# Norm statistics one unit earlier, x^T chunks and residual rows requested one at a time, last stores on three queues

## The chip, the cores and the metric

One Trainium2 chip, one of its cores. The metric is the device time of one execution in microseconds (us). Before the change it is 900.78 us, the median of three runs (899.95 to 901.37).

## The reference

The inputs are q, k and v of shape (4 batches, 8 heads, 768 positions, 64), 16 centroids for each head, and the weights of a two-layer block, all float32 by the time they are used (the block's weights arrive as float64).

```python
q_n, k_n, c_n = (t / (norm(t, axis=-1) + 1e-6) for t in (q, k, centroids))
q_assign = argmax(einsum('bhsd,hcd->bhsc', q_n, c_n), -1)
k_assign = argmax(einsum('bhsd,hcd->bhsc', k_n, c_n), -1)
scores = where(q_assign[..., :, None] == k_assign[..., None, :], q @ k^T / sqrt(64), -1e9)
x = softmax(scores) @ v                      # heads side by side: (4, 768, 512)
mu, var = mean(x, -1), mean((x - mu)**2, -1)
xn = (x - mu) / sqrt(var + 1e-6) * g_ln
out = x + maximum(xn @ w_ch1, 0) @ w_ch2     # 512 -> 2048 -> 512
```

## The kernel before

The kernel has two stages. The first, up to about 329 us of the span, is attention for 16 pairs of heads. It leaves two copies of x in device memory: transposed (`xT_d`, features by positions) and by rows (`x_d`). The change does not touch it. The second stage is the block, one batch `b` (0 to 3) after the other.

*The block.* Products with `w_ch1` (first layer) and `w_ch2` (second layer) are done with seven products of half-size blocks in place of eight, so between the TensorE products there are sums of blocks on VectorE. The first layer of a batch is cut into eight units `j` of about 9 us, each with seven products (`first_layer(b, j, part)`, its matmuls at L803). From batch 1 on the second layer does this twice over (`deep_layer`): seven outer products `m`, in the order 4, 7, 1, 6, 5, 2, 3, each of seven inner ones (`way`), makes 49 steps of 1.3 us, with the matmuls at L1093. The list `STEPS` gives their order; two ways of an outer product come after the first ways of the next: (4,1) (4,2) (4,6) (4,5) (4,7) (7,1) (7,2) (4,4) (4,3) (7,6) (7,5) (7,7) (1,1) (1,2) (7,4) (7,3) (1,6) and so on. In batch 1 deep steps begin at 544.0 us, in batch 2 at 683.9 us, in batch 3 at 820.5 us. The last two products of the first layer (parts 4 and 3 of unit 7) stand after (4,1) and (4,2).

*The weights of the deep steps* come from device memory, 256 KB for each step, through a ring of ten slots in SBUF (`ring_load`, L1035). Step number i uses slot i modulo 10. Ten loads are issued at the ends of units 5, 6 and 7 (four, four, two), and after that one load follows each step. Where a load reads from shows in the trace: `w_d` and `w_t` hold sums of blocks, `w_all` plain blocks. Steps (1,1) and (1,2) are numbers 12 and 13 and the first that read `w_all`.

*The queues.* The order of TensorE, VectorE, ScalarE and of SyncE's queue (SP) is the order of the program text, so a DMA that has to wait on SP holds all later ones. SP issues nearly all DMAs of this stage; ScalarE's queue helps only with output stores of the last batch. SP's and ScalarE's DMAs share eight semaphores in turn, so that the ninth DMA waits until the first of the nine has landed. POOL's queue is idle from about 400 us on.

*Work for batch b+1 inside batch b.* The end of unit `j` is `unit_end(b, j)`. Batch b+1's row statistics are taken there for b+1 of 2 and 3: `rows_load` (L526) fetches 128 rows of `x_d` into one of two buffers, `norm_rows` takes their mean and variance with two ScalarE passes. One of the six row tiles is done at the end of each of the units 1 to 6. `norm_stats` (end of unit 6) takes the root on ScalarE and the reciprocal on VectorE. `norm_stat_rows` (end of unit 7) turns the 12 x 128 statistics on TensorE (L569), copies them out (L573), stores them to `stat_d` (L574) and reads them back twice, spread over all partitions, as `stat_row` (L577, 384 KB each). In batch 1 `w2_split` stores a 1 MB operand to `w_d` at the end of the units 0 to 6 (L1011). Then come the ring loads of that unit's end.

In the deep layer `between()`, called after step (4,2), asks for the transposed x of batch b (`rest_load`, 768 KB, L1137), which VectorE adds to the output (`add_rest`, L1143, first used after step (4,3)), and for the four chunks of the transposed x of batch b+1 (`norm_load`, 384 KB each, L521). VectorE subtracts the mean row from chunk 0 after step (4,4), from chunk 1 after (7,5), from chunk 2 after (1,3), from chunk 3 after (6,6) (`norm_apply`, L584). The table `jobs` holds which of these calls follows which step.

*The end.* In the last batch the outer product 3 is turned and stored piece by piece. `last_part` (L1191 transposes, L1195 stores) acts after the ways 2, 7, 4 and 3, with four stores each, alternately on ScalarE's and SP's queue. After the last instruction of each engine's program come a load of a flag (L1438) and a branch (L1439) over a general path that is not taken with these inputs, and a barrier in which POOL collects the other engines (L1632).

Of the kernel before, what the change touches and what calls it, by code (L numbers as in the profile page):

```python
# [19 lines left out]
def kernel(  # L20
# [11 lines left out]
    nc = tc.nc  # L32
    B, H, S, D = q.shape
# [3 lines left out]
    NT = S // P  # L37
# [5 lines left out]
    NDC = DM // P  # L43
# [167 lines left out]
    NDH, NFH = NDC // 2, NFC // 2  # L211
# [303 lines left out]
            normed[b] = [xpool.tile([P, NDC, S], F32, tag="xn", name="xn")]  # L515
        return normed[b]

    def norm_load(b):
        xn = norm_tiles(b)[0]
        for c in range(NDC):  # L520
            nc.sync.dma_start(out=xn[:, c, :], in_=xT_d[b][c])  # L521

    def rows_load(b, t):
# [173 lines left out]
    with tc.manual_schedule(engines=order | {mybir.EngineType.Pool}):  # L697
        for u in range(len(pairs) * slots):
            n, slot = divmod(u, slots)
# [378 lines left out]
    def unit(name):  # L1078
        return units.tile([P, 2, HC], F32, tag="unit", name=name, bufs=6)
# [51 lines left out]
    def rest_load(b, k):  # L1131

        if b + 1 == B and k:
            t = xpool.tile([P, 3, S], F32, tag="sums", name="rest_x", bufs=2)[:, :2]
        else:
            t = units.tile([P, 2, S], F32, tag="rest", name="rest_x", bufs=1)
        nc.sync.dma_start(out=t, in_=xT_d[b][2 * k : 2 * k + 2].rearrange("h p s -> p h s"))  # L1137
        rest_x[b, k] = t
# [32 lines left out]
    def deep_layer(b, more, st):  # L1171

        done = {}

        def ahead_of(m):
            p = st[m] = {}
            onto = {2: 1, 3: 5}.get(m)
            p["add"] = done.get(onto)
            p["to"] = done[m] = done[onto] if onto else unit(f"m{m}")

        def sum_onto(i, j):
            nc.vector.tensor_tensor(done[i], done[i], done[j], ALU.add)

        def last_part(o, way):

            part = {2: (0, 0), 7: (1, 1), 4: (1, 0), 3: (0, 1)}.get(way)
            if part is None:
                return
            r, j = part
            y = unit("y_end")[:, 0, :QC]  # L1190
            nc.vector.transpose(y, o[:, j].rearrange("p (t a r) -> p t a r", a=2, r=Q)[:, :, r])  # L1191
            to = out[b].rearrange("(a r t) m -> a (r t) m", r=Q, t=NT)[r]
            for i in range(P // Q):
                m = MH + j * P + i * Q
                (nc.scalar, nc.sync)[i % 2].dma_start(  # L1195
                    out=to[:, m : m + Q], in_=y[i * Q : (i + 1) * Q].rearrange("r (t f) -> r t f", f=Q)
                )

        def between():
            first_layer(b, NFH - 1, 3)  # L1200
            relu(len(summed))
            outer_sums(NFH - 1, True)
            rest_load(b, 0)
            if more:
                norm_load(b + 1)
            else:
                rest_load(b, 1)

        def s4(n):
            return lambda: outer_late((1, 1), (0, 1), "s", n)  # L1210

        def norm(i, c):
            return lambda: norm_apply(b + 1, i, c)

        def rest(r, k, m):
            return lambda: add_rest(b, r, k, done[m])

        def out_of(r, k, m):
            return lambda: turn(b, r, k, done[m])

        def onto(i, j):
            return lambda: sum_onto(i, j)

        jobs = {
            (4, 1): [lambda: first_layer(b, NFH - 1, 4)],
            (4, 2): [between],
            (4, 3): [rest(1, 0, 4)],
            (7, 6): [s4(0)], (7, 4): [s4(1)], (7, 3): [s4(2)], (1, 6): [s4(3)],
            (1, 4): [onto(4, 7)], (6, 3): [onto(6, 1)],
            (5, 4): [onto(4, 6)], (5, 3): [onto(5, 6)], (2, 6): [onto(7, 5)],  # L1230
        }
        for i, m in enumerate(ORDER[1:]):
            for n, way in enumerate((5, 7)):
                jobs[ORDER[i], way] = [lambda m=m, n=n: inner_sums(st, m, (n,))]
        if more:
            for at, (i, c) in (
                ((4, 4), (0, 0)), ((7, 5), (0, 1)), ((1, 3), (0, 2)), ((6, 6), (0, 3)),
                ((6, 5), (1, 0)), ((6, 4), (1, 1)), ((5, 6), (1, 2)), ((5, 5), (1, 3)),
            ):
                jobs.setdefault(at, []).append(norm(i, c))  # L1240
            jobs[2, 4] = [out_of(1, 0, 4)]
            jobs[2, 3] = [rest(0, 0, 2), lambda: rest_load(b, 1)]
            jobs[3, 6] = [lambda: x_sum(b + 1, 1)]
            jobs[3, 5] = [lambda: w1_sums(b + 1, 0, (0, 1))]
            jobs[3, 4] = [lambda: x_sum(b + 1, 2)]
            later(
                rest(1, 1, 7), out_of(1, 1, 7), out_of(0, 0, 2), None,
                rest(0, 1, 3), out_of(0, 1, 3), None,
            )
        else:  # L1250
            jobs[1, 3] = [rest(1, 1, 7)]
            jobs[5, 6] = [rest(0, 0, 1), onto(4, 6)]
            del jobs[5, 4]
            jobs[2, 5].append(rest(0, 1, 5))
            jobs[2, 1] = [out_of(1, 0, 4)]
            jobs[2, 7].append(out_of(1, 1, 7))
            jobs[2, 3] = [out_of(0, 0, 2)]

        for m, way in STEPS:
            if way == 1:  # L1260
                ahead_of(m)
            deep_product(st, m, way)
            ring_load(b)
            leave(2 if more else 4, (nc.sync,) if more else (nc.sync, nc.scalar))
            if way == 1:
                inner_late(st, m, way)
            for job in jobs.get((m, way), ()):
                job()
            if way == 2:
                inner_late(st, m, way)  # L1270
            if m == 3 and not more:
                last_part(done[m], way)
        leave(len(leaving))
        places[1, 1], places["e"] = places["e"], places[1, 1]
# [91 lines left out]
    with tc.manual_schedule(engines=order | {mybir.EngineType.SP}):  # L1366
        first.close()
        splits = first.enter_context(tc.tile_pool(name="splits", bufs=1))
        outer = {}

        def unit_end(b, j):

            if b + 1 < B:
                if j == 0:
                    rows_load(b + 1, 1)
                elif j <= NT:
                    norm_rows(b + 1, j - 1)
            if b == 1:
                if j == 0:
                    outer["ends"] = all_in_range()  # L1380
                if j == 2:
                    outer["flag"] = flag_of(outer.pop("ends"))
                m = (1, 5, 3, 4, 2, 7, 6, None)[j]
                if m in SUMS:
                    w2_split(m, outer.pop("t"))
                elif m:
                    w2_split(m, by_half(w2_block(*{1: (0, 0), 2: (1, 0), 3: (1, 1)}[m])))
                if j in (1, 3, 5):
                    outer["t"] = w2_back({1: 4, 3: 3, 5: 2}[j])
                if j in (5, 6):  # L1390
                    outer_late("s", "e", (0, 0), j - 5)
            while pending:
                job = pending.pop(0)
                if job is None:
                    break
                job()
            if b + 1 < B and j + 2 == NFH:
                norm_stats(b + 1)
            if b + 1 < B and j + 1 == NFH:
                norm_stat_rows(b + 1)  # L1400
            leave(4)
            if j > 4:
                for _ in range(4):
                    if ring["next"] < len(STEPS) * (b - 1) + RING:
                        ring_load(b)

        for b in range(1, B):
            deep[b] = {}
            if b + 1 < B:
                rows_load(b + 1, 0)  # L1410
            if b == 1:
                outer["t"] = w2_back(1)
                first_units(b, 0)
            else:
                first_layer(b, 0, 1)
                first_layer(b, 0, 2)
                first_layer(b, 0, 6)
                relu(1)
                w1_sums(b, 0, (2, 3))
                x_sum(b, 3)  # L1420
                first_layer(b, 0, 5)
                first_layer(b, 0, 7)
                x_sum(b, 4)
                w1_sums(b, 1)
            unit_end(b, 0)
            for j in range(1, NFH):
                first_units(b, j)
                unit_end(b, j)
            relu(len(summed))
            inner_sums(deep[b], ORDER[0], cs=slice(NQH - 1, NQH))  # L1430
            if b == 1:
                first.close()
                units = pool("units", 1)
            deep_layer(b, b + 1 < B, deep[b])
        flag = outer["flag"]
# [201 lines left out]
```

## Time and profile before

| what | value |
|---|---|
| time, median of three runs | 900.78 us (899.95 to 901.37) |
| the profiled execution's own time | 897.76 us |
| its span, from first to last instruction | 896.0 us |
| TensorE busy | 879.3 us, 98% of the span |
| VectorE busy | 701.6 us, 78% |
| ScalarE busy | 400.1 us, 45% |
| POOL busy | 77.9 us, 9% |
| granted TensorE clock, mean | 0.998 |
| last matmul ends | 887.65 us |

The profiled execution is a single one, and it is 3.0 us under the median; 1.76 us of its time lies outside the span. TensorE's busy time is modelled for the ends of matmuls, but its gaps can be read: where a matmul starts later than the one before it ended, the waits name who released it. "SPq", "ACTq" and "POOLq" are the instructions of the queues of SyncE, ScalarE and POOL; their length is the time to issue a DMA, not the time to its landing. Lines are those of the kernel before.

### The profile page before, as it was taken

What the parts mean: (1) busy time and instruction counts of PE and PEld (TensorE: products, weight loads), DVE (VectorE), ACT (ScalarE), POOL (GpSimd) and SP (SyncE); (2) the same over time, 40 slices, a digit from 0 to 9 for tenths busy, and PEclk for the clock granted to TensorE, in tenths of its full rate; (3) what the DMA queues carried; (4) which work ended last, traced back from release to release, by engine and by line L of the source; (5) the groups of instructions that cost most, each with busy time, mean ns of one, the idle gap of its engine ahead of it and who ended that gap; (6) DMA issues with size and microseconds to landing.
All of it is one profiled execution on the core that took longest, in us unless ns stands there. A gap on an engine that the chain in (4) does not pass through costs nothing.

```text
span 896.0 us, 13278 instructions
## 1 busy us (share of the span) xinstructions
PE 879.3 (98%) x4724; PEld 576.4 (64%) x4724; DVE 701.6 (78%) x1158; ACT 400.1 (45%) x739; POOL 77.9 (9%) x141
## 2 busy tenths in 40 slices
PE   8999999999999999999999999899999999999996
PEld 4444444444444445568886558897557997556995
DVE  6999999999889879889545677897646897655775
ACT  4777777999877743331003552101553101333110
POOL 1122222121112112110000000000000000000000
PEclk9999999999999999999999999999999999999999
DMA  7789899999898446877513668863243872421775
GB/s 160 156 179 175 161 183 190 211 193 181 168 201 148 125 97 185 201 180 243 181 55 119 215 214 284 286 187 77 50 121 130 306 204 60 88 83 60 242 198 104
DMA packets 250841, 147.86 MB, mean 165 GB/s; under 512 B 193952, under 2 KB 209424, under 8 KB 249744
## 3 DMA queue, kind: packets, MB, share of 16 engines
q1 hardware_dynamic: 234992, 130.77, 55.8%
q0 software_dynamic: 7712, 14.99, 8.4%
q10 hardware_dynamic: 8064, 1.18, 0.8%
q8 instruction: 39, 0.64, 0.3%
q14 instruction: 34, 0.28, 0.1%
HBM read 105.25 MB, written 33.25 MB: 155 GB/s over the span
## 4 chain that ended last, share of the span: by engine, by line
PE 62%; DMA 2%; DVE 0%; SPq 0%; issue 0%; ACT 0%
PE x_ps L803 18%; PE x_ps L1093 11%; PE z_ps L803 9%; PE z_ps L1093 6%; PE x_ps L910 5%; PE y_ps L803 5%; PE y_ps L1093 3%; PE z_ps L910 2%; PE y_ps L910 1%; PE s_ps L386 1%; DMA w<-w_all 1%; PE a_ps L398 1%; DMA w<-w_d 1%; DMA stat_d<-st 0%; PE den_ps L452 0%; DVE u L1108 0%
## 5 line engine op out<-in xcount | busy, mean ns | idle before, releaser
L381 ACT ACTIVATE e<-s_ps 128x768 f32<-128x768 f32 x192 | 151.7, 812 | 9.3 <-PE s_ps L386 4.6
L386 PE MATMUL s_ps<-t,t 64*128 64x384 f32 x768 | 154.9, 483 | 0.0
L398 PE MATMUL a_ps<-e,v_sb 128*64 128x384 f32 x768 | 130.9, 491 | 0.0
L398 PEld LDWEIGHTS a_ps<-e,v_sb 128*64 128x64 f32 x768 | 52.3, 137 | 75.7 <-issue 62.8
L386 PEld LDWEIGHTS s_ps<-t,t 64*128 64x128 f32 x768 | 68.2, 188 | 35.1 <-issue 34.2
L1093 PE MATMUL x_ps<-lower,w 128*128 128x192 f32 x448 | 81.2, 327 | 3.4 <-DMA w<-w_all 2.5
L1093 PEld LDWEIGHTS x_ps<-lower,w 128*128 128x128 f32 x448 | 73.9, 190 | 5.7 <-DMA w<-w_all 2.8
L834 DVE TENSOR_TENSOR lower<-z_ps,u 128x384 f32<-128x384 f32 x56 | 31.0, 553 | 54.5 <-PE z_ps L803 45.7
L386 PE MATMUL s_ps<-mask,mask 64*128 64x384 bf16 x384 | 63.0, 324 | 1.1 <-ACT e L381 0.7
L842 ACT ACTIVATE lower<-lower 128x384 f32<-128x384 f32 x88 | 45.0, 522 | 41.2 <-DVE lower L834 41.2
L433 DVE TENSOR_TENSOR two<-e 128x1536 f32<-128x1536 f32 x30 | 52.5, 1751 | 12.9 <-ACT e L381 12.7
L829 ACT COPY u<-x_ps 128x384 f32<-128x384 f32 x64 | 30.6, 478 | 67.6 <-PE x_ps L803 67.6
L829 ACT COPY p<-x_ps 128x384 f32<-128x384 f32 x32 | 15.0, 470 | 91.2 <-PE x_ps L803 91.2
L436 DVE TENSOR_TENSOR two<-two,e 128x1536 f32<-128x1536 f32 x30 | 52.5, 1750 | 1.7
L803 PE MATMUL x_ps<-xn,w 128*128 128x384 f32 x128 | 46.6, 487 | 0.0
L803 PE MATMUL x_ps<-xn,ws 128*128 128x384 f32 x128 | 46.5, 486 | 0.0
L803 PE MATMUL z_ps<-xt,ws 128*128 128x384 f32 x128 | 46.5, 486 | 0.0
L803 PE MATMUL x_ps<-xt,ws 128*128 128x384 f32 x128 | 46.5, 486 | 0.0
L803 PE MATMUL z_ps<-xn,ws 128*128 128x384 f32 x128 | 46.5, 486 | 0.0
L803 PE MATMUL y_ps<-xn,w 128*128 128x384 f32 x128 | 46.5, 486 | 0.0
L803 PE MATMUL x_ps<-xt,w 128*128 128x384 f32 x128 | 46.5, 486 | 0.0
L386 PEld LDWEIGHTS <-mask 64*128 64x128 bf16 x384 | 19.2, 94 | 42.3 <-issue 11.3
(209 smaller groups left out, 1484.7 us busy)
## 6 DMA issues: line engine op xcount, KB each, us to landing
w<-w_d SPq DMA_DIRECT2D x84, 256.0 KB, 3.4
raw<-in_moe_w_ch_dram SPq DMA_DIRECT2D x32, 512.0 KB, 5.2
w<-w_t SPq DMA_DIRECT2D x36, 256.0 KB, 4.9
w<-tb POOLq DMA_DIRECT2D x32, 256.0 KB, 6.4
w_d<-wt SPq DMA_DIRECT2D x7, 1024.0 KB, 5.1
w<-w_all SPq DMA_DIRECT2D x27, 256.0 KB, 3.2
v_sb<-in_v_dram SPq DMA_DIRECT2D x32, 192.0 KB, 5.4
xr<-x_d SPq DMA_DIRECT2D x24, 256.0 KB, 3.0
```

Source lines behind the costliest of these rows:

```text
L381: nc.scalar.activation(e, s[:, :, :HC], AF.Exp, scale=SCALE)
L386: nc.tensor.matmul(s[:, j, :HC], of_keys[:, keys], of_queries[:, o : o + HC], start=part == first, stop=part != first, skip_group_check=True,)
L398: nc.tensor.matmul(acc[j * D : (j + 1) * D, :HC], loaded[n]["v"][:, j, c, :], e[:, j, :], start=(c == 0), stop=(c == NT - 1),)
L433: nc.vector.tensor_tensor(two, soft.pop(u), soft.pop(u + 1), ALU.add)
L436: nc.vector.tensor_tensor(two, two, soft.pop(u + 2), ALU.add)
L803: nc.tensor.matmul(bank[:, :HC], lhs[:, c, :], rhs[:, c], start=first and c == 0, stop=c == NDH - 1, skip_group_check=True,)
L829: nc.scalar.copy(t, bank[:, :HC])
L834: nc.vector.tensor_tensor(h, bank[:, :HC], other, ALU.add)
L842: nc.scalar.activation(h, h, AF.Relu)
L910: nc.tensor.matmul(bank[:, :MH].rearrange("p (h f) -> p h f", h=2), hidden[lhs + (c,)][:, tt * P : (tt + 1) * P], rhs[:, :, c], start=firs ...
L1093: nc.tensor.matmul(bank, w[:, c, :], a[:, c], start=way in (1, 2, 5) and c == 0, stop=c == NQH - 1, skip_group_check=True,)
```

## The change

1. Statistics one unit earlier. `norm_rows(b+1, j)` runs at the end of unit j in place of j+1 (0 to 5 in place of 1 to 6), `norm_stats` at the end of unit 5 in place of 6, `norm_stat_rows` at the end of unit 6 in place of 7.
2. Requests one by one. `between()` asks for chunk 0 alone. Chunk 1 is requested after step (4,7), chunk 2 after (7,2), chunk 3 after (7,3). `rest_load(b, 0)` moves from (4,2) to (4,5); in the last batch `rest_load(b, 1)` moves from (4,2) to (7,2).
3. Last stores. Of the stores of the last outer product, way 7 uses SP, ScalarE, POOL, SP and way 4 ScalarE, POOL, SP, ScalarE; ways 2 and 3 start with SP.

No arithmetic is changed. Each engine has as many instructions as before, save the two stores that go from SP and ScalarE to POOL.

```diff
-    def norm_load(b):
+    def norm_load(b, *chunks):
         xn = norm_tiles(b)[0]
-        for c in range(NDC):
+        for c in chunks or range(NDC):
             nc.sync.dma_start(out=xn[:, c, :], in_=xT_d[b][c])
...
             r, j = part
+            queues = {
+                7: (nc.sync, nc.scalar, nc.gpsimd, nc.sync), 4: (nc.scalar, nc.gpsimd, nc.sync, nc.scalar),
+            }.get(way, (nc.sync, nc.scalar))
...
-                (nc.scalar, nc.sync)[i % 2].dma_start(
+                queues[i % len(queues)].dma_start(
...
             outer_sums(NFH - 1, True)
-            rest_load(b, 0)
             if more:
-                norm_load(b + 1)
-            else:
-                rest_load(b, 1)
+                norm_load(b + 1, 0)
...
             (4, 2): [between],
+            (4, 5): [lambda: rest_load(b, 0)],
...
-                jobs[ORDER[i], way] = [lambda m=m, n=n: inner_sums(st, m, (n,))]
+                jobs.setdefault((ORDER[i], way), []).append(lambda m=m, n=n: inner_sums(st, m, (n,)))
...
+            for at, c in (((4, 7), 1), ((7, 2), 2), ((7, 3), 3)):
+                jobs.setdefault(at, []).append(lambda c=c: norm_load(b + 1, c))
...
         else:
+            jobs[7, 2] = [lambda: rest_load(b, 1)]
...
                 if j == 0:
                     rows_load(b + 1, 1)
-                elif j <= NT:
-                    norm_rows(b + 1, j - 1)
+                if j < NT:
+                    norm_rows(b + 1, j)
...
+            if b + 1 < B and j + 3 == NFH:
+                norm_stats(b + 1)
             if b + 1 < B and j + 2 == NFH:
-                norm_stats(b + 1)
-            if b + 1 < B and j + 1 == NFH:
                 norm_stat_rows(b + 1)
```

## The prediction

> **What bounds the kernel now.** First the page: TensorE is busy 98% of the span at a granted clock of 0.998, and its products are untouched. So a change can win only what TensorE waits, and the two ends. Its own waits come next (who waited for whom: us in total, times, longest):
>
> ```profile
> PE x_ps L1093 <- DMA w<-w_all: 2.5, 1, 2.5
> PE x_ps L1093 <- DVE u L1108: 1.3, 3, 0.5
> PE den_ps L452 <- ACT x L413: 1.2, 1, 1.2
> ```
>
> The list goes on with 3 us in the attention stage. One wait of 2.5 us can be touched: a weight of a deep step that came late. The other part is the tail: the last matmul ends at 887.65 us, the span at 896.0. The chain of waits from 540 to 570 us tells why that weight was late (start, us, what):
>
> ```profile
> 544.59 0.15 ACT st L573
> ...
> 544.76 4.30 DMA stat_d<-st
> ...
> 549.08 0.33 SPq L577
> ...
> 550.45 5.79 DMA w<-w_d
> ...
> 556.30 8.79 DMA w<-w_all
> ...
> 565.13 1.57 PE x_ps L1093 x8
> ```
>
> The reader sees no arithmetic in it: the statistics are copied out at 544.6, SP stores them, stands 4.3 us until they have landed, reads them back, and only then goes on to ring loads. The load for step (1,1) leaves at 556.30 and lands 8.8 us later, where `w_all` loads take 3.2 us by the page's median. SP's timeline shows what is ahead of it:
>
> ```profile
> 540.79 0.37 SPq L1011 DMA_DIRECT2D w_d<-wt  x1
> 541.26 0.46 SPq L1035 DMA_DIRECT2D w<-w_d  x1
> 541.81 2.15 SPq L1035 DMA_DIRECT2D w<-w_t  x2
> 544.05 0.43 SPq L1035 DMA_DIRECT2D w<-w_d  x1
> ...
> 551.94 0.44 SPq L1137 DMA_DIRECT2D rest_x<-xT_d  x1
> 552.43 3.42 SPq L521 DMA_DIRECT2D xn<-xT_d  x4
> 556.30 1.46 SPq L1035 DMA_DIRECT2D w<-w_all  x2
> ```
>
> Residual and four chunks are 768 + 4 x 384 = 2304 KB. The windows (span, busy engines, clock, share of the DMA engines, GB/s) say that these run full from 557 to 566 us, and again in batch 2 from 690 to 702:
>
> ```profile
> 557.00:566.00 9.00, 6.46 (x40) 6.16 (x39) 5.21 (x7) 0.95 (x3) 0.00 (x0) 1.00 1.04 399
> 690.00:702.00 12.00, 12.00 (x75) 12.00 (x75) 10.25 (x15) 1.91 (x6) 0.00 (x0) 1.00 1.03 384
> ```
>
> So 399 GB/s is all there is: 256 KB take 0.66 us, 384 KB 0.98, 768 KB 1.97. Batch 2 has the same queue but no wait: its `w_all` load left at 692.93; with 8.8 us again it lands at 701.7, and the step starts 18.5 us after the first deep step, as in batch 1, so at 702.2. Half a microsecond saved it.
>
> **The change part by part.**
>
> *Statistics one unit up.* ScalarE's six row tiles (two passes of 0.63 and 0.72 us, two reads of 0.19 us, one small one: 1.9 us each), the root (0.30 us), VectorE's two small ones (0.17 and 0.18 us), one transpose on TensorE (0.11 us) and three DMAs each move by 9 us; none is added. ScalarE is busy 45% of the span and waits on TensorE for every `u` and `p`; its rows at unit 0 need a tile fetched earlier. The `rows_load` that follows each tile waits for ScalarE one unit earlier too; behind it on SP stand `w_d` stores and output stores, which already wait longer for VectorE. Nothing for all of that; without this cover, at most 1.9 us in one unit.
>
> On SP it matters in batch 1. There `norm_stat_rows` now stands behind the 1 MB store of unit 6 (L1011 at 540.79, held by VectorE, which the change leaves there), and ahead of that unit's four ring loads, which before left at 541.3 to 544.5. The wait for `stat_d` is not removed, it is moved ahead of them. New times: the store leaves at 541.2 behind 1 MB that lands 4.3 us after its issue (the least of seven; up to 5.8 with loads behind it), so `stat_d` lands at about 545.4; in batch 2, with idle DMA engines, it took 1.3 us. The upper end is 540.79 + 5.8 + 1.3 = 547.9. Then `stat_row` twice at 545.4. Before, the second ring load behind these landed at 550.45 + 5.79 = 556.24, which is 7.2 us after the first `stat_row` (549.08); the first is one load earlier, 6.5 us. So the ring's load number 4, for step (4,7), lands at 551.9. TensorE wants it at 552.0. Later ones follow each 0.66 us against steps of 1.3 us. New wait: 0 by the middle, 2.4 us at the upper end. I take 0.2, since 4.3 us was the rule for a 1 MB store with no load behind it.
>
> *Requests one by one.* Step (1,1)'s load now has ahead of it, from 545.4, the eight ring loads 4 to 11 (the eighth lands 6.5 + 7 x 0.66 = 11.1 us after, at 556.5), chunk 0 (557.5), then itself: 558.2. TensorE wants it at 562.5, so the 2.54 us wait goes, with 4 us to spare. Next late: the residual behind step (1,2)'s load lands at about 560.8, where VectorE asks at 559 (before, VectorE waited 3.7 us for chunk 0 and came to the residual at 562.8); chunk 1 lands at 562.5, when VectorE, after two sums of 0.95 us, comes at 563.5. The sum that TensorE needs first from that queue (for step (1,6) at 567.7) is then ready at 566.4. Nothing, with 1.3 us of cover; beyond it each us late is a us. Chunks 2 and 3 are asked 6 and more steps ahead of use. In batch 2 the statistics leave 9 us earlier with idle engines (from 674 to 682 they are 1% busy), so all this has more room; saved there 0 in this execution. Batch 3 only spreads two loads: 0.
>
> *Last stores.* The tail in the timeline and by source line:
>
> ```profile
> 885.56 5.20 SPq L1195 DMA_DIRECT2D out_dram<-y_end  x6
> 885.56 5.50 ACTq L1195 DMA_DIRECT2D out_dram<-y_end  x6
> 888.08 0.38 DVE L1191 STREAM_TRANSPOSE y_end<-m 128x192 f32<-128x192 f32 x1
> ```
> ```profile
> L1439 POOLq EVENT_SEMAPHORE  x1: 17/17/17, 501.1 to 501.1; - x1
> L1439 SPq COMPARE_BRANCH  x1: 45/45/45, 890.8 to 890.8; - x1
> L1439 SPq EVENT_SEMAPHORE  x8: 17/17/17, 893.7 to 894.3; - x8
> ```
> ```profile
> L1632 POOLq DRAIN  x3: 46/107/5046, 501.2 to 895.7; - x3
> ```
>
> The last piece is turned at 888.46, but SP issues until 890.76 and ScalarE until 891.06, as each takes 0.6 us or more a store and waits for landings eight back. Then comes a branch (SP: 890.8 to 893.7, 2.9 us) and eight waits. SP and ScalarE get five stores in place of six: one issue less, 0.6 us, on both. SP's and ScalarE's ends lie within some 0.2 us, so both must come earlier, and do. I take -0.6 (bounds: 0, if landings hold it; -1.0).
>
> POOL gets two stores, the second ready at 887.16. No POOL store of this form is in the trace; nearest is `rdens<-flat`, also 128 or more short pieces, issued in 0.57 us and landed after 3.2 (the longest POOL row 6.4). [...] But a landing at 887.4 + 3.2 = 890.6, or 893.8 by the longest row, is still before SP's end of waits (894.3). More serious is what follows on POOL. Before, it took its flag and branch at 501 us, and its drain of 5.05 us cost nothing. Now these come after the stores: issued 888.1, flag 0.5, branch to 888.8, drain to 893.9. The barrier, at 895.2, would come at 894.6: hidden by 0.7 us. [...]
>
> Sum against the profiled execution: -2.54 + 0.2 - 0.6 = -2.9 us, so a span of 893.1 and a time of 894.9. The median is 3.0 us above this execution, for reasons that the trace can't show; if part of it is longer waits of the same kind (batch 2 was 0.5 us from one) the gain is more. I leave it: 900.78 - 2.9 = 897.9 us.
>
> **The rivals.**
>
> *The wait moves (chance 0.20).* `stat_d` lands nearer 547.9 and step (4,7) waits up to 2.4 us, or VectorE's queue is late by more than its 1.3 us. For it: both covers are thin, and SP's stop now falls ahead of loads that were early. Against: the 1 MB store has only the 12 short rows of the statistics behind it. It gives 899 to 900.8, 900 in the middle: no difference that can be told. A measurement of this kernel can tell about 0.2%, 1.8 us.
>
> *POOL ends the kernel (0.15, of it 0.11 slower).* Its drain begins only when its stores have landed. Place: the barrier after the last store. Price: 893.8 (longest row) + 5.05 = 898.9, then 0.8 us as before: the span ends at 899.7, +3.7, with -2.3 at step (1,1): +1.4; with a fetch of 2.9 us ahead of it +4.3. It decides from a drain that ends after 894.6, and the whole is slower than before from 897.5. For it: a 5 us drain that nothing in the trace explains. Against: that drain came 100 us after POOL's last DMA, so it waited for none. It gives 902.2 (900 where it ends early).
>
> *The change doesn't do what it says (0.05).* The late load is an accident of this execution and the runs have another 3 us elsewhere: 900.2, from the tail alone.
>
> **How the numbers follow.** My forecast 0.60: 897.9, its own range 896.3 to 899.2; some of it (0.04) falls short of 1.8 us. Faster: 0.56. Within 0.2%: that 0.04, 0.17 of the moved wait, 0.04 of POOL and 0.05: 0.30. Slower: 0.11 of POOL and 0.03 of the moved wait, if both covers fail at once: 0.14. The range takes my range with its lower end moved by 0.8 for waits in batch 2 that the runs may have, and reaches up into POOL's case: 895.5 to 901.8.
>
> **What would show it.** Right: no wait of TensorE on `w<-w_all`; `stat_d` stored at about 541.2 in batch 1 with `stat_row` at 545 to 546; VectorE's wait for `xn` gone or under 1 us; SP's branch near 890.1; POOL's drain ended before SP's waits. Wrong: a TensorE wait on `w<-w_t` or `w<-w_d` near 552, or on a VectorE sum near 568; a span that goes on more than 8.3 us after the last matmul, with POOL last.

## The result and the profile after

| | before | changed |
|---|---|---|
| time, median | 900.24 us (899.72 to 901.37) | 895.66 us (894.60 to 896.75) |
| the profiled execution's own time | 897.76 us | 896.45 us |
| its span | 896.0 us | 894.6 us |
| last matmul to the end of the span | 8.34 us | 8.73 us |

The ratio is 0.9949 (95%: 0.9936 to 0.9962), so the change is worth 4.6 us; 2.9 were predicted. The spans of the two profiled executions differ by only 1.4 us, and that sum is the first thing to read: measured between the same points of TensorE's program, batch 1's deep layer is 2.5 us shorter, the attention stage, which the change does not touch, is 0.75 us longer, and the tail is 0.39 us longer. The 0.75 is not the change's: over the ten profiles on record the first product of the block begins anywhere from 329.03 to 329.91 us, and both of these ends are executions of the changed kernel.

TensorE's waits in the changed kernel (us in total, times, longest) have no weight in them any more. Among them are

```profile
PE x_ps L1093 <- DVE u L1108: 1.3, 3, 0.5
PE den_ps L452 <- ACT x L413: 1.2, 1, 1.2
...
PE x_ps L1093 <- issue: 0.3, 1, 0.3
```

The first two stood there before. The third, 0.3 us, is all that is new in the deep layer. VectorE's waits from 545 to 572 us are moved rather than gone. Of its 3.7 us for `xn` (chunk 0) 1.1 are left, and it now waits for the residual, which landed at 562.59:

```profile
DVE m L1143 <- DMA rest_x<-xT_d: 2.1, 1, 2.1
DVE xn L584 <- DMA xn<-xT_d: 1.1, 1, 1.1
```

The chain of waits from 540 to 570 us, which ran through ScalarE, SP and three DMAs before, is now TensorE's alone:

```profile
550.11 1.30 PE x_ps L1093 x8
551.41 1.30 PE z_ps L1093 x8
552.71 2.60 PE x_ps L1093 x16
555.31 1.30 PE y_ps L1093 x8
...
560.51 1.30 PE z_ps L1093 x8
561.81 2.60 PE x_ps L1093 x16
...
568.31 0.26 issue
568.57 1.54 PE x_ps L1093 x8
```

Step (4,7) starts at 552.71 without a gap, so the wait that was feared there did not come. The gap of 0.26 us ahead of step (1,6), at 568.31, is called "issue", which means that the profile names nobody. But VectorE's sum for that step (567.51 to 568.47) ends 0.07 us before TensorE's weight load starts, and VectorE had worked with hardly a pause since the residual landed, so it is in all likelihood the late residual that reaches TensorE here:

```profile
567.51 0.96 DVE L1074 TENSOR_TENSOR lower<-qs,lower 128x768 f32<-128x768 f32 x1
...
568.54 1.27 PEld L1093 LDWEIGHTS x_ps<-lower,w 128*128 128x128 f32 x8 [0.52 <-issue]
```

SP's timeline of the same stretch (start, us, instruction) shows the new order:

```profile
541.27 0.37 SPq L1011 DMA_DIRECT2D w_d<-wt  x1
541.74 0.46 SPq L574 DMA_DIRECT2D stat_d<-st  x1
545.73 0.80 SPq L577 DMA_DIRECT2D stat_row<-stat_d  x2
546.63 0.38 SPq L1035 DMA_DIRECT2D w<-w_d  x1
...
551.46 0.34 SPq L521 DMA_DIRECT2D xn<-xT_d  x1
552.32 1.01 SPq L1035 DMA_DIRECT2D w<-w_all  x2
553.61 0.41 SPq L1137 DMA_DIRECT2D rest_x<-xT_d  x1
```

SP still stands 3.5 us (541.74 + 0.46 to 545.73) until the statistics have landed, but is through 3.3 us earlier than before (549.08), though TensorE's program is 0.75 us later in this execution. One chunk, not four and a residual, lies ahead of the two `w_all` loads. They land at 559.96 and 560.63, and step (1,1) wants its one at about 563.1.

The tail, by source line (count, shortest/median/longest in ns, first and last start). Lines stand 4 further down than in the kernel before: L1443 is the branch over the general path, L1636 the barrier.

```profile
L1443 SPq EVENT_SEMAPHORE  x8: 17/17/17, 891.3 to 891.8; - x8
...
L1443 POOLq COMPARE_BRANCH  x1: 53/53/53, 886.2 to 886.2; - x1
L1443 POOLq EVENT_SEMAPHORE  x1: 17/17/17, 886.4 to 886.4; - x1
...
L1443 SPq COMPARE_BRANCH  x1: 45/45/45, 888.4 to 888.4; - x1
```
```profile
L1636 POOLq EVENT_SEMAPHORE  x4: 17/17/17, 893.8 to 894.5; - x4
L1636 POOLq DRAIN  x3: 46/107/7274, 886.5 to 894.3; - x3
L1636 SPq DRAIN  x3: 7/7/13, 892.7 to 894.0; - x3
```

The last matmul ends at 885.86. SP's branch comes 2.55 us after it; before it was 3.16: the store that was taken from SP is gained. But SP, ready for the barrier at 892.7, has to wait. POOL's first drain begins at 886.5 and lasts 7.27 us, to 893.8, and only then does POOL's barrier go on. POOL closes the kernel, 1.1 us after SP was ready.

### The profile page after: what moved, and what is told of

The parts are those of the page before. It is cut to its first block, busy times and chain, and to the rows that moved or that the text cites. A ratio compares the mean times of both kernels' runs of the same rounds, so it can differ in the third digit from the quotient of the medians.

```text
span 894.6 us, 13278 instructions
## 1 busy us (share of the span) xinstructions
PE 879.7 (98%) x4724; PEld 576.6 (64%) x4724; DVE 701.5 (78%) x1158; ACT 399.7 (45%) x739; POOL 79.3 (9%) x143
## 4 chain that ended last, share of the span: by engine, by line
PE 64%; DVE 0%; issue 0%
PE x_ps L803 18%; PE x_ps L1093 12%; PE z_ps L803 9%; PE z_ps L1093 6%; PE x_ps L910 5%; PE y_ps L803 5%; PE y_ps L1093 3%; PE z_ps L910 2%; PE y_ps L910 1%; PE s_ps L386 1%; PE a_ps L398 1%; PE den_ps L452 0%; DVE u L1108 0%; DVE y_end L1194 0%; DVE m L1108 0%
```

## The experiments

Where did the other 1.7 us of the gain come from, and what is each part worth? "Before" is in each case the kernel before in the same session: 899.20 us (31 executions) for the first four kernels in the order of the record (before_again, stats_only, requests_only, no_pool), 899.04 us (24 executions) for the other four. The ratio given with each is not made from the two medians alone and can differ from their quotient by some 0.1%. (One of the expectations speaks of another chip; the record names the same one for both sessions.)

**before_again: the kernel before, profiled once more.** No edit. It asks what the 3.0 us between the median and the profiled execution are.

> The kernel before, run once more to see another execution of it. The profiled execution of before was 3.0 us under its median. Theory 'longer waits': most executions have more of the wait for w_all than the 2.5 us that was profiled, in batch 1 or also in batch 2, where the load came 0.5 us ahead of need; then an execution near 900 us shows 4 to 6 us of TensorE waits on weights. Rival 'elsewhere': the waits on weights stay near 2.5 us and the 3 us lie in the attention stage or in the two ends.

Measured: 899.61 us (ratio 1.0001, 0.9979 to 1.0022); the profiled execution took 899.75 us, with a span of 898.0, 2.0 us over the first profile's. The same wait is there, no longer than before. Step (1,1) in TensorE's timeline:

```profile
561.02 1.46 PE L1093 MATMUL x_ps<-lower,w 128*128 128x192 f32 x8
565.00 2.88 PE L1093 MATMUL x_ps<-lower,w 128*128 128x192 f32 x8 [2.52 <-DMA w<-w_all]
567.67 1.87 PE L1093 MATMUL y_ps<-lower,w 128*128 128x192 f32 x8
569.38 1.46 PE L1093 MATMUL x_ps<-lower,w 128*128 128x192 f32 x8
```

The eight products behind the wait take 2.88 us; in the first profile of the same kernel they took 1.57. The windows (start:end, length, TensorE busy with the number of its products in brackets, granted clock, DMA share, GB/s) say why:

```profile
561.67:565.08 3.41, 0.90 (x6) 1.00 1.04 389
565.08:568.49 3.41, 3.41 (x11) 0.50 1.05 385
568.49:571.90 3.41, 3.41 (x23) 1.00 0.69 221
```

The number behind the bracket is the clock. It is halved from 565.08 to 568.49, for 3.41 us. In the first profile it stays at 1.00 behind the same wait:

```profile
560.57:563.98 3.41, 2.01 (x13) 1.00 1.04 396
563.98:567.40 3.42, 2.27 (x14) 1.00 1.05 385
```

The second step behind (1,1) starts 569.38 - 565.00 = 4.38 us after it, before 2.70: 1.68 us are lost. So the wait had a second price in this execution and not in the first: 1.7 us more, of the 2.0 by which the spans differ. Neither longer waits on weights nor a loss elsewhere accounts for more than the other 0.3.

The windows are not cut at random. In this trace the clock changes at 565.08, at 568.49 and, after the program's last product, at 892.76: 327.68 us from the first to the last, which is 96 times 3.413, with the second 3.41 us behind the first. The first profile's clock changes only once, at 891.66, and its windows above are cut in steps of 3.413 us back from there. That these steps also hold in a trace with a single change is the author's assumption. Whether the clock falls can then be compared with how busy TensorE was in the window before, as the profile models it. It fell after windows with 0.90 us of products (above), 1.10 us (at the end of pool_way7) and 1.17 us (at the end of requests_only). It did not fall after one with 1.47 us (stores_only, whose wait for `w_all` was 2.10 us), nor after one with more. First the end of requests_only, then the wait in stores_only with the window behind it:

```profile
885.63:889.05 3.42, 1.17 (x8) 1.00 0.37 60
889.05:892.46 3.41, 0.00 (x0) 0.50 0.27 46
```
```profile
561.05:564.46 3.41, 1.47 (x10) 1.00 1.04 390
564.46:567.88 3.42, 3.27 (x20) 1.00 1.06 387
```

The two executions of the kernel before differ in where the gap falls. In before_again it lay within one window; in the first profile a border at 563.98 cut it in two. In these rows 1.94 us without products (3.41 - 1.47) in one window were not followed by the half clock, and 2.24 us (3.41 - 1.17) were. If the limit always lay between these two, which was not shown, a gap of 2.5 us that falls at random would pass it in about four to six of ten executions (the author's estimate from the rows above).

The record also has the mean granted clock of each execution, so this can be counted. In every profile the clock is halved for the last 3.5 to 6.7 us of the span, behind the last product, which alone gives means of 0.998 to 0.996; 3.41 us at half clock in the middle, of a span of 898.0, take another 0.002 by the same count. Of the 63 executions of the kernel before in the two sessions, 28 have 0.997 or 0.998, and their mean time is 898.0 us. The 35 with 0.996 or less have 900.2 us (in 15 of them, at 0.996, the end alone could be the reason). Of the 25 executions of the three kernels with both part 1 and part 2 (the changed one, no_pool, pool_way7), 24 have 0.997 or 0.998. The mean of all 63 is 899.2 us, so by this count the clock costs about 1.2 us on the average, an estimate that puts the whole difference down to it.

**stats_only: part 1 alone.**

```diff
-                elif j <= NT:
-                    norm_rows(b + 1, j - 1)
+                if j < NT:
+                    norm_rows(b + 1, j)
...
-            if b + 1 < B and j + 2 == NFH:
+            if b + 1 < B and j + 3 == NFH:
                 norm_stats(b + 1)
-            if b + 1 < B and j + 1 == NFH:
+            if b + 1 < B and j + 2 == NFH:
                 norm_stat_rows(b + 1)
```

> The statistics one unit earlier, and nothing else. Theory 'queue of bytes': the residual and four chunks, 2304 KB, are still asked for ahead of step (1,1)'s load, so it lands at about 563.1 in the profiled execution's time and TensorE still waits some 0.6 us; 1.9 us gained there and more in batch 2, so -2 to -4 us against before. Rival 'SP's stop is the whole cause': the wait is gone and the gain is that of both parts, -5 us.

Measured: 896.91 us, ratio 0.9975 (0.9962 to 0.9987), 2.3 us less. The statistics move as in the full change (`stat_d` at 541.78, `stat_row` at 545.76), but the residual and four chunks still lie ahead of the `w_all` load. From the chain:

```profile
555.64 8.66 DMA w<-w_all
564.30 0.04 issue
564.35 1.57 PE x_ps L1093 x8
```

The load leaves at 555.64 and again takes 8.66 us (8.79 before), so 1.4 us of waiting are left, where 0.6 were expected. Ordering it earlier gained only what SP gained, 1.2 us; the length of the transfer hardly changed. The remaining 1.1 us of the median are not in the wait itself. The clock can account for them: the wait of 1.4 us is shorter than the 1.94 us without products after which it did not fall in stores_only, and 9 of the 12 executions have a mean clock of 0.997 or 0.998 (of before 14 of 31). Among these alone the two kernels differ by 1.0 us (896.8 against 897.8), about what the wait lost.

**requests_only: part 2 alone.**

```diff
-            rest_load(b, 0)
             if more:
-                norm_load(b + 1)
-            else:
-                rest_load(b, 1)
+                norm_load(b + 1, 0)
...
+            (4, 5): [lambda: rest_load(b, 0)],
...
+            for at, c in (((4, 7), 1), ((7, 2), 2), ((7, 3), 3)):
+                jobs.setdefault(at, []).append(lambda c=c: norm_load(b + 1, c))
...
+            jobs[7, 2] = [lambda: rest_load(b, 1)]
```

> The chunks and residual rows requested one by one, and nothing else: statistics and stores as before. Theory 'queue of bytes': 4 ring loads and one chunk ahead of step (1,1)'s load, which lands at about 559 against a need at 562.5; no wait for weights in batch 1 or 2, and the whole gain of both parts, -5 us against before. Rival 'SP's stop': the stop of 4.3 us for the statistics in front of the loads still makes one late, TensorE waits 1 us or more, gain under 3 us.

Measured: 896.48 us, ratio 0.9970 (0.9954 to 0.9985), 2.7 us less where 5 were expected. No weight is waited for, with the statistics where they were. What is new is small, at two places behind step (1,1):

```profile
567.54 1.57 PE L1093 MATMUL z_ps<-lower,w 128*128 128x192 f32 x8 [0.21 <-DVE m L1108]
569.51 1.54 PE L1093 MATMUL x_ps<-lower,w 128*128 128x192 f32 x8 [0.41 <-issue]
```

Here the sums on VectorE that were forecast as next late are late, by 0.6 us in all. (The second wait is again an "issue" that ends 0.1 us after a sum of VectorE, L1074, and VectorE had waited 2.1 us for the residual.) Part 2 alone therefore removes the wait and gives back 0.6 us; with part 1 only the 0.26 us at 568.3 are left. The two parts overlap: 2.3 and 2.7 us alone, not 5 together. One of the 12 executions took 902.08 us at a mean clock of 0.995; no trace of it is on record, so where its clock fell is open.

**no_pool: parts 1 and 2, the last stores as before.** The edit is shown against the changed kernel.

```diff
-            queues = {
-                7: (nc.sync, nc.scalar, nc.gpsimd, nc.sync), 4: (nc.scalar, nc.gpsimd, nc.sync, nc.scalar),
-            }.get(way, (nc.sync, nc.scalar))
+            queues = (nc.scalar, nc.sync)
```

> The change without its third part: the last stores alternate on ScalarE's and SP's queues as before. Theory 'POOL ends the kernel': POOL's drain ended at 893.8 us in the changed kernel while SP was through at 892.7, so without POOL's stores the end is set by SP again, 8.3 us after the last matmul as before in place of 8.7: 0.4 us faster than the changed kernel, so about -5.0 us against before (the changed kernel was at -4.6). Rival 'three queues help': one store less on SP and ScalarE is worth 0.6 us, and this kernel is at -4.0 us.

Measured: 895.93 us, ratio 0.9954 (0.9939 to 0.9969), with the last matmul 8.06 us before the end of the span of 893.4. That is 3.3 us less by the medians and 4.1 by the ratio (2.8 to 5.5), so it can't tell the two expectations, -5.0 and -4.0, apart. Nearly all of the change's gain is in parts 1 and 2.

**filled_wait: the wait stays, TensorE does not idle in it.** Products whose result nobody uses are put into the kernel before, ahead of step (1,1) of batch 1.

```diff
+            if (b, m, way) == (1, 1, 1):
+                fill = ps("fill_ps")
+                for _ in range(5):
+                    nc.tensor.matmul(fill[:, :HC], ident, w1[:, 0, :HC], start=True, stop=True)
```

> The kernel before, with five matmuls whose result nobody reads (128x384 float32, 0.49 us each, 2.4 us in all) put on TensorE ahead of step (1,1) of batch 1, where it waits for its weight. Nothing else is moved; the weight still lands at about 565 us. Theory 'the wait costs the clock too': an idle TensorE lets the granted clock fall to half for 3.4 us in some executions (seen once, from 565.0 us), so the same wait with TensorE busy costs only its 2.5 us: times come as close together as those without a wait, median near 897.9, some 1.5 us under before, though nothing is taken out. Rival 'clock or not, the time goes elsewhere': the median stays that of before, within 0.3 us, or is more by what the matmuls delay.

Measured: 898.84 us, ratio 0.9997 (0.9987 to 1.0007): the median is not lower by the 1.5 us that were expected, and by its number alone this is the rival's case. The spread is smaller: the times run from 898.01 to 899.61, before's from 896.90 to 901.34, with a standard deviation of 0.5 against 1.2. TensorE's timeline shows that the filling was too long:

```profile
561.23 1.46 PE L1093 MATMUL x_ps<-lower,w 128*128 128x192 f32 x8
562.53 3.39 PE L1265 MATMUL fill_ps<-w,ident 128*128 128x384 f32 x10
565.75 1.46 PE L1093 MATMUL x_ps<-lower,w 128*128 128x192 f32 x8
```

The five products, ten in the trace, take 565.75 - 562.53 = 3.22 us in place of 2.4, and step (1,1) starts 4.52 us after the step ahead of it; in the kernel before it was 4.01. So the filling itself costs 0.5 us and takes away what the clock costs in some executions: the slow end of the times is gone and so is the fast end. Allowing for the 0.5, the median fell by 0.7 us. The clock on record agrees: 10 of the 11 executions have a mean of 0.997 or 0.998, against 12 of the 24 of before, and these 10 are 0.7 us slower than those 12 (898.9 against 898.1), about what the filling costs. In the profiled execution the clock stays at 1.00 from 555 to 572 us. So the wait with TensorE busy in it did not lose the clock here. A filling of the right length, which would show the price without this correction, was not run.

**stores_only: part 3 alone.**

```diff
+            queues = {
+                7: (nc.sync, nc.scalar, nc.gpsimd, nc.sync), 4: (nc.scalar, nc.gpsimd, nc.sync, nc.scalar),
+            }.get(way, (nc.sync, nc.scalar))
...
-                (nc.scalar, nc.sync)[i % 2].dma_start(
+                queues[i % len(queues)].dma_start(
```

> The last stores on three queues, and nothing else. Theory 'POOL ends the kernel': the wait for w_all of 2.5 us is still there, and the end is 0.4 us later, so +0.4 us against before. Prediction on record for this part: -0.6 us.

Measured: 898.19 us, ratio 0.9999 (0.9983 to 1.0015): nothing that can be told. In its barrier (L1635 here) SP and POOL stand like this:

```profile
L1635 POOLq DRAIN  x3: 46/107/7066, 887.8 to 895.4; - x3
L1635 SPq DRAIN  x3: 7/7/13, 894.3 to 895.1; - x3
```

POOL's drain ends at 887.8 + 7.07 = 894.9, 0.6 us after SP is ready at 894.3. The tail is 8.53 us, before 8.34: 0.2 us longer, not 0.6 shorter.

**after_again: the changed kernel once more.** No edit.

> The changed kernel, once more, on the chip that runs the other three. Expected -4 us against before (-4.6 by the first measurement, -3.3 for its parts 1 and 2 on another chip). Its POOL drain should again end about 4.9 us after the landing of POOL's second store and close the span.

Measured: 895.15 us, ratio 0.9958 (0.9944 to 0.9972), tail 8.67 us. In the barrier:

```profile
L1636 POOLq DRAIN  x3: 46/107/7213, 885.2 to 893.0; - x3
L1636 SPq DRAIN  x3: 7/7/13, 891.6 to 892.7; - x3
```

885.2 + 7.21 = 892.4 against 891.6: POOL closes the kernel again, by 0.8 us. Its second store landed at 887.69, so the drain ended 4.75 us after the landing; 4.9 were expected.

**pool_way7: the changed kernel with both of POOL's stores in the earlier piece.**

```diff
-                7: (nc.sync, nc.scalar, nc.gpsimd, nc.sync), 4: (nc.scalar, nc.gpsimd, nc.sync, nc.scalar),
+                7: (nc.sync, nc.gpsimd, nc.scalar, nc.gpsimd),
```

> The changed kernel with POOL's two stores both taken from way 7 (1.6 us earlier than the second of them now), none from way 4; SP and ScalarE have as many stores as in the changed kernel, one more of them late. Theory 'the drain counts from the landing': POOL's stores land about 1 us earlier than before, at about 888.0, the drain ends at 892.9, as SP's waits do: 0.9 us faster than the changed kernel. Rival 'the drain doesn't matter, the last landings do': same time as the changed kernel within 0.3 us.

Measured: 895.35 us, ratio 0.9958 (0.9943 to 0.9974), tail 8.04 us.

```profile
L1636 POOLq DRAIN  x3: 46/107/7641, 885.1 to 893.3; - x3
...
L1636 SPq DRAIN  x3: 7/7/13, 892.5 to 893.0; - x3
```

The last matmul ends at 885.5 here. The drain begins 0.4 us before that (after_again: 0.6 us behind its last matmul) and ends 0.2 us after SP is ready in place of 0.8. The tail is 0.6 us shorter, as short as with no store on POOL at all; the medians don't tell the three versions apart, so the 0.9 us that were expected can't be seen in them, nor the rival's "no difference" be refused.

The traces settle what the drain counts from. In all four profiles with last stores on POOL it ends 4.75 us after POOL's second store has landed, and the span ends 0.83 us after the drain:

| | second store landed | drain ended | span ended | landing, from the last matmul | tail |
|---|---|---|---|---|---|
| stores_only | 890.09 | 894.84 | 895.66 | 2.95 | 8.53 |
| after | 889.02 | 893.77 | 894.59 | 3.16 | 8.73 |
| after_again | 887.69 | 892.44 | 893.26 | 3.10 | 8.67 |
| pool_way7 | 888.00 | 892.75 | 893.58 | 2.47 | 8.04 |

So the end of the drain hangs on the landing, as the theory had it (888.0 and 892.9 were expected in pool_way7), and each tail is the landing and 5.57 us. In the six profiles without last stores on POOL the drain took 5.05 us, long before the end. Stores on POOL still further ahead were not tried.

## Why the prediction was right, and where it was not

*The wait for `w_all`, -2.54: right.* It is gone, and the times on the way were 541.74 for the store of `stat_d` (541.2 predicted), 545.73 for `stat_row` (545.4) and 559.96 for the landing (558.2, the step with the largest error; a cover of 4 us was forecast, 3 were there). (The block starts 0.75 us late in this execution. But for that the first two would be 0.2 and 0.4 us early, and the third 1.0 us late.) requests_only shows that the chunks were the heavier part: without them the wait is gone even with the statistics late.

*The new wait at (4,7), +0.2: right in its mechanism and rightly small.* The 1 MB store landed 4.31 us after its issue, as taken, and nothing was waited for. Of "the wait moves" the first form did not come. The second did, but small: the thin cover on VectorE's side tore, for 0.26 us ahead of 568.57, and for 0.6 us where part 2 stood alone. The residual was forecast to land at 560.8 and landed at 562.59, and the sum that was to be ready at 566.4 was ready at 568.47; the cover was 1.3 us. VectorE's wait for `xn` is 1.1 us, not gone and not quite under 1 us. A TensorE wait on a VectorE sum near 568 was one of the signs of being wrong that the prediction named.

*"The median is 3.0 us above this execution, for reasons that the trace can't show ... I leave it": this is the term that was mis-sized.* It was put at nothing, and the wait was priced from one execution, in which TensorE went on at full clock. before_again has the same 2.5 us followed by 3.4 us at half clock, 1.7 us more. With the whole price, 2.5 to 4.2 us, less the 0.26 us of new wait, the gain of parts 1 and 2 comes to 2.3 to 3.9; no_pool measured 3.3 by the medians and the full change 3.9 to 4.6. The guess on the spare room of batch 2 was not what was missing: its waits on weights did not appear in the second profile either. Three things say that the clock is. The mean clock is 0.996 or less in 35 of 63 executions of before, and in 1 of 25 with both parts. Among executions with a mean clock of 0.997 or 0.998 alone, no_pool is 2.2 us under before (895.6 against 897.8, same session) and after_again 2.7 (895.4 against 898.1), which is about the wait's own 2.54 less 0.26; what goes beyond that in the medians goes with the clock. And idle products in the gap did away with the slow executions. The spread of the times (standard deviation) is 0.6 us in no_pool, 0.9 in after_again and 1.2 and 1.6 in the two sessions of before, but also 1.7 in requests_only, by its one execution of 902 us. What is not shown: a half clock behind this wait was seen directly in one of the two profiled executions of before, the rest is from means over whole executions.

*The last stores, -0.6: mis-sized; it is 0 within what can be measured.* SP did come 0.6 us earlier, and POOL went on 0.2 us after its branch (886.2 to 886.4), as it had before, where SP took 2.9 us (888.4 to 891.3; before 890.8 to 893.7). POOL's branch and its next instruction before:

```profile
L1439 POOLq COMPARE_BRANCH  x1: 45/45/45, 500.9 to 500.9; - x1
L1439 POOLq EVENT_SEMAPHORE  x1: 17/17/17, 501.1 to 501.1; - x1
```

But the drain was taken at 5.05 us, measured where POOL had had nothing to do for 100 us. Behind two fresh stores it took 7.1 to 7.6 us in four profiles, as it ends 4.75 us after the second landing, and its end passed SP's. This is the mechanism of "POOL ends the kernel", and its sign came: a tail of 8.73 us, over 8.3, with POOL last. The size is not that of its longest case, since the stores landed 3.2 to 4.0 us after their issue, not 6.4: in the changed kernel POOL was through 1.1 us after SP, which took back the 0.6 us that SP had gained and 0.4 more. No run shows the term of 2.9 us that this rival's price calls a fetch: the 2.9 us are SP's, from its branch to its next instruction, what filled them was not shown, and POOL took 0.2 us there.

*The sum.* -2.9 was built from the terms -2.54, +0.2 and -0.6. The medians have -3.3 from the first two with the clock (no_pool), -3.9 to -4.6 for the whole change, and about 0 from the third: two errors of opposite sign. That 895.66 us still lies in the predicted range (895.5 to 901.8), though under the forecast's own (896.3 to 899.2), is luck. The lower end had been moved down by 0.8 us for longer waits in batch 2, which no run showed, and the clock, for which the prediction had no room, took their place.

## What to carry to other kernels

A short idle gap of TensorE may cost more than its length (here 2.52 us of waiting were followed by a loss of 1.68 us in one of two profiled executions): before pricing it, read the granted clock right behind it in more than one profiled execution, compare the mean clocks of all executions, and take a profile that is some us under the median as a sign that something in it comes and goes. Where a queue is blocked behind a wait, large transfers that are needed one by one should be asked for one by one: behind the residual and four chunks the load for step (1,1) left at 555.64 us and landed after 8.66 (stats_only), behind one chunk it left at 552.32 and landed after 7.6 (the changed kernel). An engine that is given the last stores may also be given a longer way to the barrier: look at what its drain takes behind work of its own, not behind idleness. Here POOL's drain took 7.07 to 7.64 us behind two stores, against 5.05 without, and ran until 4.75 us after its last landing.

## What the runs showed of the hardware that was not expected

- TensorE without a product for 2.52 us was followed by 3.4 us at half the clock in one execution of the kernel before; 2.54 us at the same place in another execution were not. In windows of 3.413 us, the distance of the clock's changes in the first of these two, the fall came after one with 0.90 us of products, and the two windows that shared the wait in the other execution had 2.01 and 2.27. In other profiles the clock fell after windows with 1.10 us (pool_way7) and 1.17 (requests_only) and not after one with 1.47 (stores_only).
- POOL's drain at the end took 5.05 us with nothing issued for a long time (six profiles), and 7.07, 7.21, 7.27 and 7.64 us behind two small stores of its own, in four profiles: each time it ended 4.75 us after the second store's landing.
- In the changed kernel POOL's two last stores took its queue 0.58 us each, no more than the same stores on SP (0.57 to 0.61) or ScalarE (0.58 to 1.00), and landed after 4.0 and 3.4 us:

```profile
884.04 0.58 POOL L1198 DMA_DIRECT2D out_dram<-y_end  x1 [483.91 <-DMA out_dram<-y]
...
885.66 0.58 POOL L1198 DMA_DIRECT2D out_dram<-y_end  x1 [1.04 <-DVE y_end L1194]
```
